# Attention's first chunks in a new order, and state updates issued earlier, in a fused attention and mixture-of-experts kernel

## The chip, the cores and the metric

The kernel runs on one core of a Trainium2 chip, as one program. The metric is the device time of one execution in microseconds (us); a profiled execution gives its own time and, beside it, the span from its first to its last instruction.

## What is computed

Three layers run one after the other. The first is a gated linear attention over 4 batches, 8 heads, 768 steps and heads of 48; its output is 3072 rows of 384. Each row then either skips the second layer or goes to one of 8 experts, and a third layer is applied to all rows.

```python
f = 1.0 / (1.0 + np.exp(-f_logit))
for t in range(S):                                   # attention
    state = f[:, :, t, :, None] * state + k[t] (x) v[t]
    y[:, :, t] = q[:, :, t] . state
out = x                                              # experts, for rows with x @ w_skip > 0
out[i] = x[i] + gate_w[i] * (np.maximum(x[i] @ w1[e], 0) @ w2[e]),   e = argmax(x[i] @ w_gate)
h = x @ w_in; sp = log1p(exp(min(h, 20))) (h where h > 20)           # last layer
return (h * np.tanh(sp)) @ w_out
```

## The kernel before

**Units.** The function `attention` cuts the 24 stretches of 128 steps (6 for each batch) into chunks n = 0 to 23, and each chunk into two halves of two head pairs. A unit d = 2n + h2, 0 to 47, is one such half. All engines get their instructions in the order in which the code stands; each engine works its own queue in order and waits where a tile that it needs is not ready.

**A chunk's preparation**, for all pairs at once: the sigmoid of the gate logits (`sigmoid`, ACT, in place in the tile fb, for three chunks at a time; hh counts these groups of three), then the running product of the gates over the 128 or 384 steps (`scan`, DVE, L303; `chain` joins a chunk of the first group to the one ahead of it and scans its four pairs), then on ACT a logarithm and an exponential (`recip`, L347 and L348: g = 1/e), on DVE three operations (`kg`, two of them, L356 and L357, and `kh`, L364), and on POOL the scaled queries (`qh`, L370). The tile g lies in PSUM and has one buffer. Sigmoid and logarithm are of different tables of ACT, and a change of table (`table`, L656) is an instruction.

**A unit's work.** `stage1(d)` multiplies on PE (tile at, L386) scaled queries and keys and at once turns the keys, copies on ACT and masks either on POOL (`through_act` true: ACT copies all of at into the tile am, L396, and POOL masks it, L399) or on DVE (false: ACT copies the turned keys, L404, and DVE masks the rest, L405). `stage2(d)` makes on PE the outputs (tile ou: L430 from the state tile sbd, L438 from am) and the addition to the state (L450). `evac(d)` copies the outputs on ACT (tile xts, L482). `state(d)` adds on DVE to the state tile (L471, L473 and L475, or L477), and `stage2(d + 2)` needs its result. `finalize(n)` (tile fin, L494) turns a finished chunk and makes its routing numbers.

**Order.** The loop over d issues `state(d - 1)`, the preparation of a chunk that lies ahead, `stage1(d + 2)`, `finalize`, `stage2(d)`, `evac(d)`. Sigmoids and scans of later groups stand at units listed in SIGMOID_AT and SCAN_AT. At units 15, 29, 37, 44 and 46 (the table `group`) `route1` picks experts for a group of chunks with eight small operations on DVE; some units later `rank` counts on PE, `rank_read` takes the counts, `route2_all` makes row numbers, and POOL scatters one chunk's rows per unit (L229). `keep_warm(n)` issues n matmuls of which nothing is used (L664): 25 at the start, 3 after `stage2(0)`, 14 at unit 2. The experts' layers follow the attention, in functions that this change leaves as they are.

```python
SIGMOID_AT = {4: (2, 3), 12: (4, 5), 22: (6, 7)}
SCAN_AT = {4: ((2, 3), (5, 7)), 12: ((3, 5), (7, 9)), 22: ((3, 5), (7, 9))}
group = [(0, 7, 15, 2), (7, 7, 29, 2), (14, 4, 37, 2), (18, 3, 44, 1), (21, 2, 46, 1)]
```

Of the kernel before, what the change touches and what calls it, by code (L numbers as in the profile page):

```python
# [45 lines left out]
WARM = 25  # L46
# [8 lines left out]
LOAD_AT = 24  # L55

# [180 lines left out]
def attention(tc, A, st, weights, open_weights, first_x):  # L237
# [67 lines left out]
    def chain(c):  # L305
        nc.vector.tensor_tensor(d1[0][:, :, c * CH], fb[0][:, :, c * CH], fb[0][:, :, c * CH - 1], ALU.mult)
        for p in range(NP):
            scan(0, p, c, c + 1)
# [34 lines left out]
    def recip(n, parts=1):  # L343
        l = wk.tile([128, NP, CH], F32, name="l", tag="l", bufs=2)[K112]
        g = pr.tile([128, NP, CH], F32, name="g", tag="ut", bufs=1)[K112]
        for ps in pair_parts(parts):
            nc.scalar.activation(out=l[:, ps], in_=e_of(n)[:, ps], func=AF.Ln)  # L347
            nc.scalar.activation(out=g[:, ps], in_=l[:, ps], func=AF.Exp, scale=-1.0)  # L348
        k = wk.tile([128, NP, CH], F32, name="kg", tag="kg", bufs=2)[K112]
        gs[n] = (g, k)  # L350

    def kg(n, ps=slice(0, NP)):
        hh, c3 = divmod(n, 3)
        sl = slice(c3 * CH, (c3 + 1) * CH)
        g, k = gs[n]
        nc.vector.tensor_tensor(k[:, ps], kq[hh % 2][:, 0, ps, sl], g[:, ps], ALU.mult)  # L356
        nc.vector.tensor_tensor(g[:, ps], e_of(n)[:, ps], g[:, ps], ALU.mult)  # L357

    def kh(n, ps=slice(0, NP)):
        g, k = gs[n]  # L360
        if prep[n][1] is None:
            prep[n][1] = wk.tile([128, NP, CH], F32, name="kh", tag="kh", bufs=3)[K112]
        o = prep[n][1]
        nc.vector.scalar_tensor_tensor(o[:, ps], g[:, ps], 2.0, k[:, ps], ALU.subtract, ALU.mult, reverse0=True)  # L364

    def qh(n):
        hh, c3 = divmod(n, 3)
        sl = slice(c3 * CH, (c3 + 1) * CH)
        q = qi[n % 4][K112]
        nc.gpsimd.tensor_tensor(q[:, :, 0:CH], kq[hh % 2][:, 1, :, sl], e_of(n), ALU.mult)  # L370
        prep[n] = [q, None, vb[hh % 3][:, c3, :]]
# [3 lines left out]
    def stage1(d, through_act):  # L375
# [17 lines left out]
        m = part(am, 0, CH)  # L393
        if through_act:
            if keys:
                nc.scalar.copy(am, at)  # L396
            else:
                nc.scalar.copy(m, part(at, 0, CH))
            nc.gpsimd.affine_select(  # L399
                m, m, pattern=[[0, 2], [0, 2], [1, CH]], compare_op=ALU.is_ge, fill=0.0, base=0, channel_multiplier=-1  # L400
            )
        else:
            if keys:
                nc.scalar.copy(part(am, CH, QW), part(at, CH, QW))  # L404
            nc.vector.tensor_tensor(  # L405
                m, part(at, 0, CH), const["mask"].rearrange("p (j a) t -> p j a t", j=2), ALU.mult
            )
        ats[d] = am
# [6 lines left out]
    def stage2(d):  # L415
# [3 lines left out]
        am = ats.pop(d)  # L419
# [26 lines left out]
        if c < NC - 1:  # L446
            for a in range(2):
                for j in range(2):
                    p = 2 * h2 + a
                    nc.tensor.matmul(  # L450
                        ut[64 * j:64 * j + D, a, j * D:(j + 1) * D],
                        lhsT=am[:, j, a * QW + CH:(a + 1) * QW],
                        rhs=vt[:, (2 * p + j) * D:(2 * p + j + 1) * D], start=True, stop=True,
                        skip_group_check=True,
                    )

    def state(d):
        n, h2 = divmod(d, 2)
# [232 lines left out]
    nc.gpsimd.memset(d1[1], E_FLOOR)  # L691
# [27 lines left out]
    for d in range(ND):  # L719
# [5 lines left out]
        fresh = h2 == 0 and 0 < n < NT - 2 and d - 2 not in SIGMOID_AT  # L725
# [3 lines left out]
        if d > 0:  # L729
# [50 lines left out]
        if d == 0:  # L780
            ends(0)
            sigmoid(1, 0, 2)
            sigmoid(1, 2, 4)
            table(LN_EXP)
            starts(1, nc.gpsimd)
            recip(2)
            qh(2)
        if d == 1:
            scan(1, 0)
# [6 lines left out]
            const.update(route_consts(tc, st["cp"], wk))  # L796
        if d % 6 == 1 and d // 6 + 2 < NH:
# [800 lines left out]
```

## Time and profile before

| | us |
|---|---|
| median of 3 runs | 736.2 (733.36 to 737.27) |
| the profiled execution's own time | 732.49 |
| its span | 730.6 |
| PE busy | 692.6 |
| DVE busy | 539.6 |
| ACT busy | 501.2 |
| POOL busy | 170.5 |

The profiled execution was quicker than all three timed runs. The mean granted clock of TensorE over it was 0.972 of full speed. A busy PE says little by itself, since a matmul takes about twice as long at half the clock; the rows below have the granted clock beside the busy time. The attention takes the time up to about 165 us.

### The profile page before, as it was taken

The numbers are of one execution on the slowest core, as the hardware profiler recorded it, in microseconds if no ns is written. First come the engines' busy times: TensorE is split into PE (matmuls) and PEld (weight loads), VectorE is DVE, ScalarE is ACT, GpSimd is POOL, SyncE is SP. The second block draws the span as 40 slices with busy tenths as digits, with TensorE's granted clock in tenths as the row PEclk, the third lists the DMA queues.
The fourth block names the chain that finished last, engine by engine and source line by source line (L and its number), as shares of the span: only waits on it lengthen the run. The fifth ranks groups of instructions, "written<-read, shape, count | busy, mean of one in ns | idle before, by whom it ended". The sixth has DMA issues, their size and how long they took to land.

```text
span 730.6 us, 13087 instructions
## 1 busy us (share of the span) xinstructions
PE 692.6 (95%) x5020; PEld 624.9 (86%) x5021; DVE 539.6 (74%) x1083; ACT 501.2 (69%) x858; POOL 170.5 (23%) x226
## 2 busy tenths in 40 slices
PE   7889798888999999999999999999999999999995
PEld 3678687766999999988899899989989989988994
DVE  7699967985778888969989875666666656666571
ACT  5689675654666663379889867767777676667681
POOL 6644765653011111122223120200020002001002
PEclk8899988899999999999999999999999999999998
DMA  9999844244778974532223022212142224100001
GB/s 210 257 265 273 289 152 130 99 171 147 265 251 272 297 260 149 162 133 72 101 57 118 4 83 87 87 43 87 44 139 79 65 99 141 44 1 23 22 1 47
DMA packets 39286, 95.52 MB, mean 131 GB/s; under 512 B 3540, under 2 KB 28160, under 8 KB 39216
## 3 DMA queue, kind: packets, MB, share of 16 engines
q1 hardware_dynamic: 35120, 82.71, 37.7%
q0 software_dynamic: 4096, 11.90, 4.3%
q8 instruction: 41, 0.67, 0.4%
q14 instruction: 29, 0.24, 0.1%
HBM read 79.53 MB, written 15.84 MB: 131 GB/s over the span
## 4 chain that ended last, share of the span: by engine, by line
PE 81%; DVE 10%; ACT 4%; issue 2%; POOL 1%; DMA 0%; POOLq 0%; ACTq 0%; DVEq 0%
PE y L1130 27%; PE h L1080 27%; PE y L927 9%; PE h L912 8%; DVE fb L303 3%; PE at L386 2%; PE pt L871 2%; PE ou L438 1%; PE h L941 1%; PE fin L494 1%; DVE kh L364 1%; DVE kg L356 1%; DVE g L357 1%; PE ou L430 1%; ACT L656 1%
## 5 line engine op out<-in xcount | busy, mean ns | idle before, releaser
L1094 ACT ACTIVATE sp<-hs 128x512 f32<-128x512 f32 x96 | 59.7, 628 | 72.9 <-DVE hs L1093 72.0
L1080 PE MATMUL h<-wB,wB 128*128 128x512 f32 x432 | 109.1, 397 | 0.0
L1080 PE MATMUL h<-wB,wA 128*128 128x512 f32 x432 | 107.2, 394 | 0.0
L1130 PE MATMUL y<-wD,gh 128*128 128x384 f32 x384 | 98.0, 336 | 0.0
L1130 PE MATMUL y<-wA,gh 128*128 128x384 f32 x384 | 97.7, 335 | 0.0
L1111 DVE TENSOR_TENSOR hs<-hs,sp 128x512 f32<-128x512 f32 x96 | 69.8, 727 | 32.9 <-ACT sp L1105 32.8
L1080 PEld LDWEIGHTS h<-wB,wA 128*128 128x128 f32 x432 | 80.2, 188 | 14.5
L1080 PEld LDWEIGHTS h<-wB,wB 128*128 128x128 f32 x432 | 79.5, 188 | 14.6
L1093 DVE COPY hs<-h 128x512 f32<-128x512 f32 x71 | 48.8, 688 | 40.6 <-PE h L1080 40.4
L1113 DVE TENSOR_TENSOR gl<-hs,gh 128x512 fp32r<-128x512 f32 x96 | 67.3, 701 | 13.1 <-PE y L1130 6.2
L1130 PEld LDWEIGHTS y<-wA,gh 128*128 128x128 f32 x384 | 70.0, 188 | 4.3 <-ACT stage L1149 0.2
L1130 PEld LDWEIGHTS y<-wD,gh 128*128 128x128 f32 x384 | 70.0, 188 | 3.7
L1130 PE MATMUL y<-wD,gl 128*128 128x384 f32 x192 | 64.6, 336 | 0.0
L1130 PE MATMUL y<-wA,gl 128*128 128x384 f32 x192 | 64.5, 336 | 0.0
L1101 ACT ACTIVATE sp<-sp,tiny 128x512 f32<-128x512 f32 x96 | 61.8, 713 | 0.3
L386 PE MATMUL at<-qi,kh 48*128 48x176 f32 (+1 forms) x384 | 44.1, 352 | 10.2 <-DVE lg L502 5.9
L1105 ACT ACTIVATE sp<-sp 128x512 f32<-128x512 f32 x96 | 52.9, 621 | 0.3
L229 POOL DMA_INDIRECT out<-stage,idx x24 | 23.6, 984 | 125.6 <-ACT stage L1149 62.0
L1112 DVE CAST gh<-hs 128x512 fp32r<-128x512 f32 x96 | 48.8, 508 | 3.3
L900 ACT ACTIVATE mhh<-h 128x256 fp32r<-128x256 f32 x64 | 24.6, 384 | 38.4 <-PE h L912 29.7
L386 PEld LDWEIGHTS at<-qi,kh 48*128 48x128 f32 x384 | 31.5, 204 | 15.8 <-POOL am L399 5.4
L229 POOL DMA_INDIRECT tokens<-rows x14 | 15.4, 1098 | 107.1 <-DVE rows L960 104.9
(233 smaller groups left out, 1461.0 us busy)
## 6 DMA issues: line engine op xcount, KB each, us to landing
stage<-in_w SPq DMA_DIRECT2D x64, 768.0 KB
kq<-in_kqT SPq DMA_DIRECT2D x6, 1344.0 KB
rows<-tokens SPq DMA_DIRECT2D x18, 388.0 KB
fb<-in_fT SPq DMA_DIRECT2D x7, 672.0 KB
vb<-in_v SPq DMA_DIRECT2D x7, 576.0 KB
tokens<-zeros SPq DMA_DIRECT2D x4, 776.0 KB
kq<-in_kqT SPq DMA_DIRECT2D x4, 448.0 KB
kq<-in_kqT SPq DMA_DIRECT2D x1, 896.0 KB
```

The lines of the kernel that those rows point to most:

```text
L386: nc.tensor.matmul(at[:, j, a * QW:a * QW + w], lhsT=k[r, p, :], rhs=q[r, p, 0:w], start=True, stop=True)
L912: nc.tensor.matmul(h, lhsT=w[:, o:o + 128], rhs=x[:, k, :], start=(k == 0 and i == 0), stop=(k == KD - 1 and i == 2),)
L927: nc.tensor.matmul(ys[e, a], lhsT=h, rhs=w[:, ws], start=(f == 0 and i == 0), stop=(f == NE - 1 and i == 2),)
L1080: nc.tensor.matmul(h, lhsT=w[:, o:o + 128], rhs=x[:, k, :], start=(k == 0 and i == 0), stop=(k == KD - 1 and i == 2),)
L1093: (nc.scalar.copy if busy(s) else nc.vector.tensor_copy)(hs, h)
L1094: nc.scalar.activation(out=sp, in_=hs, func=AF.Sigmoid, scale=-1.0)
L1101: nc.scalar.activation(out=sp, in_=sp, func=AF.Ln, bias=st["tiny"])
L1105: nc.scalar.activation(out=sp, in_=sp, func=AF.Tanh, scale=-1.0)
L1111: nc.vector.tensor_tensor(hs, hs, sp, ALU.mult)
L1112: nc.vector.tensor_copy(gh, hs)
L1113: nc.vector.tensor_tensor(gl, hs, gh.bitcast(F32), ALU.subtract)
L1130: nc.tensor.matmul(ys[b][a], lhsT=g[:, a * 128:(a + 1) * 128], rhs=w, start=(first and i == 0), stop=(fs[-1] + 1 in ends and i == len(ins) ...
```

## The change

It rearranges the start: chunk 1 is scanned and prepared in two halves of two pairs, the first units' products stand ahead of the second half, the sigmoids of group 1 stand between the copies of unit 2 and unit 0, and chunk 2's scans behind `state(0)`. Units 0 and 2 to 5 (OUT_FIRST) issue `stage2(d)` ahead of `stage1(d + 2)`. The turned keys of units masked on DVE get a tile of their own, kt. The matmuls of `keep_warm` become 18, 4 and 12, and the last stand at unit 3 between `stage2(3)` and `stage1(5)`. At units with scans of later groups `state(d)` is issued between the two scans, and at routing units ahead of `route1`; the call at the next unit then does nothing. The load of the routing weights wg moves ahead of chunk 1's keys on SP's queue, the filling of d1[1] and the building of finw change places on POOL. The line numbers of the changed kernel are 1 to 28 higher.

```diff
@@ constants
-WARM = 25
+WARM = 18
+OUT_FIRST = (0, 2, 3, 4, 5)

-    def chain(c):
-        nc.vector.tensor_tensor(d1[0][:, :, c * CH], fb[0][:, :, c * CH], fb[0][:, :, c * CH - 1], ALU.mult)
-        for p in range(NP):
+    def chain(c, pairs=range(NP)):
+        ps = slice(pairs[0], pairs[-1] + 1)
+        nc.vector.tensor_tensor(d1[0][:, ps, c * CH], fb[0][:, ps, c * CH], fb[0][:, ps, c * CH - 1], ALU.mult)
+        for p in pairs:
             scan(0, p, c, c + 1)
...
-    def recip(n, parts=1):
...
+    def recip(n, which=(slice(0, NP),)):
...
-    def qh(n):
+    def qh(n, ps=slice(0, NP)):
...
         else:
             if keys:
-                nc.scalar.copy(part(am, CH, QW), part(at, CH, QW))
+                kt = wk.tile([128, 2, 2, D], F32, name="kt", tag="kt", bufs=2)
+                nc.scalar.copy(kt, part(at, CH, QW))
...
-                        lhsT=am[:, j, a * QW + CH:(a + 1) * QW],
+                        lhsT=kt[:, j, a, :],
...
     def state(d):
+        if d not in ous:
+            return
...
     def keep_warm(n):
+        wps = pr.tile([128, 512], F32, name="wps", tag="fin", bufs=1)
...
+    wg = load_gate(tc, A["wg9"], wk)
     load_kq(0, 1, 2)
     load_v(0, 1, 2)
-    wg = load_gate(tc, A["wg9"], wk)
...
-    nc.gpsimd.memset(d1[1], E_FLOOR)
+    pairs = pair_parts(2)
...
-    recip(0, 2)
-    chain(1)
+    recip(0, pairs)
+    chain(1, range(0, 2))
     qh(0)
-    for pp in pair_parts(2):
+    const.update(gate_consts(tc, wg, const["ident"], wk))
+    for pp in pairs:
         kg(0, pp)
         kh(0, pp)
-    recip(1)
-    qh(1)
+    recip(1, pairs[0:1])
+    qh(1, pairs[0])
+    stage1(0, False)
+    stage1(1, True)
+    chain(1, range(2, 4))
+    recip(1, pairs[1:2])
+    qh(1, pairs[1])
+    for pp in pairs:
+        kg(1, pp)
+        kh(1, pp)
     table(SIGMOID)
-    stage1(0, False)
     sigmoid(0, 0, NP, 2, 3)
-    kg(1)
-    kh(1)
-    stage1(1, True)
-    const.update(gate_consts(tc, wg, const["ident"], wk))
-    chain(2)
-    for c in (1, 2):
-        nc.gpsimd.memset(d1[0][:, :, c * CH], E_FLOOR)
+    nc.gpsimd.memset(d1[1], E_FLOOR)
...
-        fresh = h2 == 0 and 0 < n < NT - 2 and d - 2 not in SIGMOID_AT
+        fresh = h2 == 0 and 1 < n < NT - 2 and d - 2 not in SIGMOID_AT
...
-        if d > 0:
+        if d > 1:
             state(d - 1)
...
-        if 0 < d and d + 2 < ND:
-            if d == 2:
-                keep_warm(14)
+        ahead = d in OUT_FIRST
+        if d == 1:
+            stage1(3, False)
+        elif not ahead and d + 2 < ND:
             stage1(d + 2, all(d - i not in SIGMOID_AT for i in (1, 2)))
...
         stage2(d)
         if d == 0:
-            keep_warm(3)
-            stage1(2, True)
+            keep_warm(4)
+            stage1(2, False)
+            sigmoid(1, 0, 2)
...
         evac(d)
+        if ahead and d > 0:
+            if d == 3:
+                keep_warm(12)
+            stage1(d + 2, True)
...
                     scan(hh, p)
+                    state(d)
                     scan(hh, p + 1)
...
         if d == 0:
-            ends(0)
-            sigmoid(1, 0, 2)
             sigmoid(1, 2, 4)
             table(LN_EXP)
             starts(1, nc.gpsimd)
+            state(0)
+            chain(2)
+            for c in (1, 2):
+                nc.gpsimd.memset(d1[0][:, :, c * CH], E_FLOOR)
             recip(2)
             qh(2)
+            ends(0)
         if d == 1:
+            state(1)
             scan(1, 0)
...
+        if d == 2:
+            recip(3)
+            qh(3)
+            kg(3)
+            kh(3)
...
             if d == r[2]:
+                state(d)
                 route1(*r[0:2])
```

DVE's queue just behind chunk 0's preparation. Before (d is the scan's second operand, fb the running product, sbd the state):

```order
L405 TENSOR_TENSOR am<-at,mask 128x4x128
L356 TENSOR_TENSOR kg<-kq_100,g 112x512
L357 TENSOR_TENSOR g<-fb_102,g 112x512
L364 SCALAR_TENSOR_TENSOR kh<-g,kg 112x512
L306 TENSOR_TENSOR d_113<-fb_102 112x4
L303 SCALAR_TENSOR_TENSOR fb_102<-fb_102,d_113 112x128 x4
L471 COPY sbd_118<-ou_124 112x4x48
L303 SCALAR_TENSOR_TENSOR fb_103<-fb_103,d_114 112x384 x2
```

and now:

```order
L412 TENSOR_TENSOR am<-at,mask 128x4x128
L308 TENSOR_TENSOR d_113<-fb_102 112x2
L304 SCALAR_TENSOR_TENSOR fb_102<-fb_102,d_113 112x128 x2
L359 TENSOR_TENSOR kg<-kq_100,g 112x256
L360 TENSOR_TENSOR g<-fb_102,g 112x256
L367 SCALAR_TENSOR_TENSOR kh<-g,kg 112x256
L359 TENSOR_TENSOR kg<-kq_100,g 112x256
L360 TENSOR_TENSOR g<-fb_102,g 112x256
L367 SCALAR_TENSOR_TENSOR kh<-g,kg 112x256
L412 TENSOR_TENSOR am<-at,mask 128x4x128
L480 COPY sbd_118<-ou_124 112x4x48
```

Chunk 1's three operations are six of half the size behind the scans of its last two pairs, the mask of unit 2 has come to DVE, and chunk 2's scans stand behind the first state copy.

PE's queue from unit 2 on. Before, behind the 14 unused matmuls (at is `stage1`, fin is `finalize`, ou is `stage2`):

```order
L664 MATMUL wps<-warm 128x512
L386 MATMUL at<-qi_121,kh 128x176 x4
L494 MATMUL fin<-finw,xts_115 64x105 x8
L430 MATMUL ou_124<-qi_120,sbd_118 64x128 x4
L438 MATMUL ou_124<-am,vb_110 48x128 x4
L450 MATMUL ou_124<-vb_110,am 48x48 x4
L386 MATMUL at<-qi_121,kh 128x176 x4
```

and now, behind `stage2(1)`; eleven more pairs of the last kind follow, and then `stage1(5)`:

```order
L457 MATMUL ou_125<-vb_110,am 48x48 x4
L503 MATMUL fin<-finw,xts_115 64x105 x8
L437 MATMUL ou_124<-qi_120,sbd_118 64x128 x4
L445 MATMUL ou_124<-am,vb_110 48x128 x4
L457 MATMUL ou_124<-vb_110,kt 48x48 x4
L391 MATMUL at<-qi_121,kh 128x176 x4
L437 MATMUL ou_125<-qi_120,sbd_118 64x128 x4
L445 MATMUL ou_125<-am,vb_110 48x128 x4
L457 MATMUL ou_125<-vb_110,kt 48x48 x4
L673 LDWEIGHTS warm
L673 MATMUL wps<-warm 128x512
```

Each `stage2` now stands ahead of the `stage1` that it followed, and the unused matmuls stand ahead of `stage1(5)`.

DVE's queue at unit 29, a unit with scans and routing. Before (mx to oh is `route1`):

```order
L303 SCALAR_TENSOR_TENSOR fb_109<-fb_109,d_114 112x384 x2
L540 TENSOR_REDUCE mx<-lg 128x7
L541 TENSOR_SCALAR comp<-lg 128x7
L542 TENSOR_TENSOR rt<-lg,mx 128x56
L543 TENSOR_TENSOR ex<-lg,mx 128x56
L544 SCALAR_TENSOR_TENSOR rt<-rt,iota 128x56
L545 TENSOR_REDUCE mn<-rt 128x7
L546 TENSOR_TENSOR rt<-rt,mn 128x56
L547 TENSOR_TENSOR oh<-rt,comp 128x56
L473 TENSOR_TENSOR ou_125<-ou_125,sbd_117 112x192
L475 TENSOR_TENSOR sbd_118<-ou_125,f_978 112x4x48
L356 TENSOR_TENSOR kg<-kq_101,g 112x512
```

and now:

```order
L304 SCALAR_TENSOR_TENSOR fb_109<-fb_109,d_114 112x384
L482 TENSOR_TENSOR ou_125<-ou_125,sbd_117 112x192
L484 TENSOR_TENSOR sbd_118<-ou_125,f_987 112x4x48
L304 SCALAR_TENSOR_TENSOR fb_109<-fb_109,d_114 112x384
L549 TENSOR_REDUCE mx<-lg 128x7
L550 TENSOR_SCALAR comp<-lg 128x7
L551 TENSOR_TENSOR rt<-lg,mx 128x56
L552 TENSOR_TENSOR ex<-lg,mx 128x56
L553 SCALAR_TENSOR_TENSOR rt<-rt,iota 128x56
L554 TENSOR_REDUCE mn<-rt 128x7
L555 TENSOR_TENSOR rt<-rt,mn 128x56
L556 TENSOR_TENSOR oh<-rt,comp 128x56
```

The two operations of `state(29)` (ou, sbd) have moved up past eight routing operations and the second scan.

## Rows read from the trace of the kernel before

**Rows 1.** Windows: busy us (count) of PE, PEld, DVE, ACT, POOL; granted clock, DMA.
```profile
128.00:146.00 18.00, 15.49 (x221) 13.74 (x217) 16.72 (x46) 12.57 (x26) 11.83 (x14) 0.81 0.28 98
...
250.00:730.60 480.60, 470.90 (x2535) 431.58 (x2533) 340.17 (x604) 332.41 (x527) 59.08 (x65) 0.99 0.26 86
```

**Rows 2.** Windows of PE alone: length, busy us (count), granted clock, DMA share, GB/s.
```profile
14.50:16.30 1.80, 1.43 (x16) 0.50 1.17 239
28.00:30.00 2.00, 2.00 (x25) 0.50 1.09 236
32.00:40.00 8.00, 7.76 (x132) 1.00 1.08 260
114.00:118.00 4.00, 4.00 (x66) 0.50 0.91 235
```

**Rows 3.** DVE in order of time in the opening: start, us, what.
```profile
4.83 1.65 DVE L303 TENSOR_TENSOR_SCAN fb<-fb,d 112x128 f32<-112x128 f32 x4
...
6.78 2.40 DVE L303 TENSOR_TENSOR_SCAN fb<-fb,d 112x128 f32<-112x128 f32 x4
9.10 0.39 DVE L356 TENSOR_TENSOR kg<-kq,g 112x256 f32<-112x256 f32 x1
...
13.84 0.69 DVE L405 TENSOR_TENSOR am<-at,mask 128x512 f32<-128x512 f32 x1 [2.43 <-ACT am L404]
...
24.56 0.66 DVE L356 TENSOR_TENSOR kg<-kq,g 112x512 f32<-112x512 f32 x1
...
26.46 1.79 DVE L303 TENSOR_TENSOR_SCAN fb<-fb,d 112x384 f32<-112x384 f32 x2
...
29.59 0.69 DVE L356 TENSOR_TENSOR kg<-kq,g 112x512 f32<-112x512 f32 x1 [1.08 <-ACT g L348]
...
34.70 0.69 DVE L356 TENSOR_TENSOR kg<-kq,g 112x512 f32<-112x512 f32 x1 [0.81 <-ACT g L348]
```

**Rows 4.** ACT in order of time in the opening.
```profile
11.51 0.60 ACT L348 ACTIVATE g<-l 112x512 f32<-112x512 f32 x1 [1.66 <-DVE kh L364]
...
13.42 0.32 ACT L404 COPY am<-at 128x192 f32<-128x192 f32 x1
...
31.98 0.74 ACT L396 COPY am<-at 128x704 f32<-128x704 f32 x1 [0.62 <-PE at L386]
...
33.40 0.63 ACT L347 ACTIVATE l<-fb 112x512 f32<-112x512 f32 x1
```

**Rows 5.** PE in order of time in the opening.
```profile
16.36 1.06 PE L664 MATMUL wps<-warm 128*128 128x512 bf16 x2 [0.33 <-issue]
...
21.20 3.20 PE L664 MATMUL wps<-warm 128*128 128x512 bf16 x14
26.69 0.87 PE L386 MATMUL at<-qi,kh 48*128 48x176 f32 x8 [2.29 <-DVE kh L364]
```

**Rows 6.** DVE in order of time, from unit 29 to unit 35.
```profile
107.27 2.87 DVE L303 TENSOR_TENSOR_SCAN fb<-fb,d 112x384 f32<-112x384 f32 x2
...
112.02 0.36 DVE L475 TENSOR_TENSOR sbd<-ou,f 112x192 f32<-112x192 f32 x1
...
115.76 0.16 DVE L602 TENSOR_TENSOR pos<-pos,ou 128x7 f32<-128x7 f32 x1 [0.69 <-ACT xts L482]
...
123.15 0.36 DVE L477 TENSOR_TENSOR sbd<-ou,sbd 112x192 f32<-112x192 f32 x1 [1.32 <-ACT xts L482]
124.31 0.69 DVE L356 TENSOR_TENSOR kg<-kq,g 112x512 f32<-112x512 f32 x1 [0.81 <-ACT l L347]
...
128.75 0.69 DVE L356 TENSOR_TENSOR kg<-kq,g 112x512 f32<-112x512 f32 x1 [1.70 <-ACT g L348]
```

**Rows 7.** PE in order of time, behind units 29 and 37.
```profile
112.44 0.66 PE L430 MATMUL ou<-qi,sbd 112*64 112x128 f32 x8 [1.83 <-DVE sbd L475]
...
136.60 0.79 PE L430 MATMUL ou<-qi,sbd 112*64 112x128 f32 x8 [1.99 <-DVE sbd L471]
```

**Rows 8.** POOL in order of time: the first scatter of the second group.
```profile
121.37 1.06 POOL L229 DMA_INDIRECT tokens<-xr,slot  x1 [0.99 <-DVE cs L632]
```

More of the change, by code (lines that the diff above doesn't have):

```diff
@@ L341, in attention @@
     gs = {}
-    def recip(n, parts=1):
-        l = wk.tile([128, NP, CH], F32, name="l", tag="l", bufs=2)[K112]
-        g = pr.tile([128, NP, CH], F32, name="g", tag="ut", bufs=1)[K112]
-        for ps in pair_parts(parts):
+    def recip(n, which=(slice(0, NP),)):
+        if n not in gs:
+            l = wk.tile([128, NP, CH], F32, name="l", tag="l", bufs=2)[K112]
+            g = pr.tile([128, NP, CH], F32, name="g", tag="ut", bufs=1)[K112]
+            gs[n] = (g, wk.tile([128, NP, CH], F32, name="kg", tag="kg", bufs=2)[K112], l)
+        g, _, l = gs[n]
+        for ps in which:
             nc.scalar.activation(out=l[:, ps], in_=e_of(n)[:, ps], func=AF.Ln)
             nc.scalar.activation(out=g[:, ps], in_=l[:, ps], func=AF.Exp, scale=-1.0)
-        k = wk.tile([128, NP, CH], F32, name="kg", tag="kg", bufs=2)[K112]
-        gs[n] = (g, k)
     def kg(n, ps=slice(0, NP)):
@@ L354, in kg @@
         sl = slice(c3 * CH, (c3 + 1) * CH)
-        g, k = gs[n]
+        g, k, _ = gs[n]
         nc.vector.tensor_tensor(k[:, ps], kq[hh % 2][:, 0, ps, sl], g[:, ps], ALU.mult)
@@ L359, in kh @@
     def kh(n, ps=slice(0, NP)):
-        g, k = gs[n]
+        g, k, _ = gs[n]
         if prep[n][1] is None:
@@ L369, in qh @@
         q = qi[n % 4][K112]
-        nc.gpsimd.tensor_tensor(q[:, :, 0:CH], kq[hh % 2][:, 1, :, sl], e_of(n), ALU.mult)
+        nc.gpsimd.tensor_tensor(q[:, ps, 0:CH], kq[hh % 2][:, 1, ps, sl], e_of(n)[:, ps], ALU.mult)
+        if n in prep:
+            return
         prep[n] = [q, None, vb[hh % 3][:, c3, :]]
@@ L393, in stage1 @@
         m = part(am, 0, CH)
+        kt = part(am, CH, QW)
         if through_act:
@@ L407, in stage1 @@
             )
-        ats[d] = am
+        ats[d] = (am, kt)
     ous = {}
@@ L418, in stage2 @@
         q, _, vt = prep[n]
-        am = ats.pop(d)
+        am, kt = ats.pop(d)
         ou = oub[d % 2]
@@ L457, in state @@
     def state(d):
+        if d not in ous:
+            return
         n, h2 = divmod(d, 2)
@@ L659, in attention @@
     nc.vector.memset(warm, 0.0)
-    wps = pr.tile([128, 512], F32, name="wps", tag="fin", bufs=1)
     def keep_warm(n):
+        wps = pr.tile([128, 512], F32, name="wps", tag="fin", bufs=1)
         for i in range(n):
```

## Prediction

> **What bounds the kernel now.** I read the windows over all engines first. From 250 us to the end PE is busy in 470.90 of 480.6 us at a granted clock of 0.99 [rows 1]: the experts' layers are PE at its pace, and this change leaves them alone. Inside the attention it is otherwise. From 128 to 146 us PE is busy for 15.49 of 18 us, but at a clock of 0.81, and DVE for 16.72 [rows 1]. There the end is set by waits that go round PE, ACT and DVE, and by PE's clock. So what the change is worth is what it takes from the attention's length; the rest then starts that much earlier.
>
> Two kinds of places matter. In the opening, chunk 2's `kg` starts at 24.56, chunk 3's at 29.59, chunk 4's at 34.70 [rows 3]. I use these three as posts: from `kg` follow `kh`, `stage1` and all of a unit. Further on, the timeline of PE shows two long idle stretches ended by DVE's state operations: 1.83 us until 112.44 and 1.99 us until 136.60 [rows 7]. The granted clock drops to 0.50 after the first, all through 114 to 118 us [rows 2].
>
> **The opening, part by part.** I work to each post in the new order.
>
> *Chunk 0.* Two of chunk 1's four scans (2.40 us for four) go behind chunk 0's `kg` [rows 3], which can start up to 1.2 us earlier; its six half-size operations last from 9.10 until ACT is released at 11.51, so 2.4 us [rows 3, 4]. I take `kh` done at 10.6 instead of 11.5. The copy that unit 0's mask waits for ran at 13.42, behind an exponential of 0.60 that began at 11.51 and a table change; the mask had waited 2.43 us [rows 3, 4]. The table change now stands behind it, so mask and `stage2(0)` come some 2.3 us earlier. By itself this buys nothing, because `stage1(2)` needs chunk 1's `kh`.
>
> *To chunk 2's `kg`.* DVE's queue from 10.6 holds three masks of 0.69, six short scans of 0.4 to 0.6 (four lasted 1.65, and 2.40 beside POOL), six half operations of 2.4 in all, two state operations of 0.36 and two long scans of 1.79 to 2.87 [rows 3, 6]: 9.4 to 11.7 us. It also waits three times: for the first copy of turned keys (an exponential of 0.60 and a copy of 0.32 less what DVE has in hand, say 0.9); for the second half of chunk 1's logarithm and exponential (half of the size, taken as 0.4 each, and a little to start: 0.9); and, before unit 3's mask, for chunk 2's logarithm, exponential and the copy behind them (0.63 + 0.60 + 0.32 = 1.55) [rows 4]. Sum of waits 3.3, so `kg` at 10.6 + 12.7 to 15.0 = 23.3 to 25.6, before 24.56. I take 24.2, below the middle, since the pair of long scans no longer has chunk 2's `qh` on POOL beside it; that now runs while DVE waits.
>
> *To chunk 3's.* The distance was 29.59 - 24.56 = 5.03. The second state operation no longer stands between (0.36) [rows 3, 6]: 29.59 becomes about 28.9.
>
> *To chunk 4's.* Before, 5.11 us passed between the posts. Its exponential cannot start before chunk 3's `kh`, since g has one PSUM buffer: three operations of 0.69 and one of 0.60 make 2.7, the floor. But ACT's queue has the copy of unit 5 ahead of the logarithm, as before (31.98, which waited for PE, then the logarithm at 33.40 [rows 4]), and unit 5's `stage1` now has the 12 unused matmuls ahead of it. PE: chunk 2's `kh` at 24.2 + 2.0 = 26.2, `stage1(4)` 0.87, `stage2(3)` taken as 0.9 (as `stage1`), the 12 matmuls, `stage1(5)` 0.87. Fourteen such matmuls lasted 3.20, so 12 last 2.74 [rows 5]. `stage1(5)` ends at 31.6; copy 0.74, logarithm 0.63, exponential 0.60 [rows 4] put `kg` at 33.6 to 33.8 instead of 34.70. **Term: -1.0.** Bounds: with the floor alone 28.9 + 2.7 = 31.6, so -3.1. With the 12 at the cost of the pair at 16.36 (0.53 each, at a clock of 0.50 [rows 2, 5]) they last 6.4, so +2.6. I take the 14's price, as these too follow PE work after an idle stretch.
>
> The 7 matmuls fewer at the start cost nothing: PE then waits for chunk 0's `kh`. The routing weights' load ahead of chunk 1's keys delays those by a few small packets, while `kh` of chunk 1 waits for ACT anyway; finw and the filling of d1[1] lie in POOL's idle time, and the fill is ahead of the sigmoids that its reader waits for. Uncovered, a late fill would delay the long scans by its length.
>
> *The separate tile kt* would let DVE mask while ACT copies, if the tile am were all that ties them: the mask had waited 2.43 us for that copy [rows 3]. Both read the same PSUM tile, and in the new program the mask still waits for ACT. [...] Without that tie the first mask could start about 1 us earlier, and `kg` of chunk 2 no more than that. I count 0.
>
> **State ahead of scan and routing.** At unit 29 DVE runs two scans from 107.27 for 2.87 us, eight routing operations, and then the state's two, the second at 112.02 [rows 6]. `stage2(31)` waits for it, 1.83 us, until 112.44 [rows 7]; the first scan ended early in the 2.87 and unit 29's addition was there, so the state could be done by about 109.0. PE then never stops, and need not fall to 0.50. What follows: DVE's read of the counts had waited 0.69, a state operation 1.32, chunk 19's `kg` 0.81 and chunk 20's 1.70, all for ACT behind PE [rows 6]. Those are 4.5 us of DVE idle, and no more than these can go. Against it, `rank` needs the routing's result, which now comes 0.36 + 0.36 later relative to the scans, and the scatters start behind `route2_all`: POOL had waited only 0.99 us for the first, at 121.37 [rows 8]. So bounds -1.0 (POOL sets the pace) to -4.5. I take the DVE waits up to chunk 19's `kg`, 0.69 + 1.32 + 0.81 = 2.8, and 0.3 of chunk 20's: **term -3.1**.
>
> At unit 37 the 1.99 us of PE go too, but DVE is busy for 16.72 of 18 us in 128 to 146 [rows 1] and will not end sooner for that: 0, between -1.5 and 0. Elsewhere a state operation between scans delays the next logarithm by 0.36, three times, and at unit 44 `rank` by as much; a state that is ready earlier gives a like amount back: 0, within 0.7.
>
> **Sum.** 732.49 - 1.0 - 3.1 = 728.4 for the profiled execution. That one was 3.7 us quicker than the median of the runs, 736.2, so a median of **732.1**. I call under 0.5% (3.7 us) no change, about what such runs can tell.
>
> **The rivals.**
> *A, the forecast*, 730.5 to 734: 0.42. Two thirds of it lie beyond 0.5%.
> *B, both terms at their good end and unit 37 too.* PE never drops its clock in either place: -3.1 - 4.5 gives 728.6, with unit 37 727. For it: no row shows a drop where PE had no long idle stretch. Against it: the new opening leaves PE idle while chunk 2's scans run. 0.17, faster.
> *C, given back.* The scatters hold POOL, whose next `qh` and masks stand behind them, so unit 29 gains its 1.0 only, and the opening 0 to 1: 734 to 735.5. For it [rows 8], against it that only the first scatters have no slack. 0.24, no change.
> *D, slower: the unused matmuls at half clock.* Place: PE's queue at unit 3. Between `stage2(1)`, by my working near 18 us, and chunk 2's `kh` at 26 PE has little to do; before, it was idle for 2.29 us ahead of 26.69 and the clock was 0.50 from 28 us on [rows 2, 5]. At 0.53 each the 12 cost 2.6 us more than before's post, and PE is busy for 7.76 of 8 us behind them [rows 2], so half of what follows at half clock is paid as well: over 6 us of it 3 more. 736.2 + 2.6 + 3 - 3.1 = 738.7. It decides if the clock is still 0.50 when the matmuls end. 0.17: two thirds of it slower, the rest within 0.5%. [...]
>
> **Chances.** Faster 0.28 + 0.17 = 0.45; no change 0.14 + 0.24 + 0.06 = 0.44; slower 0.11. Range: from B's 727 to D's lower half, 738.
>
> **What would show it.** Right: PE without idle time at units 30 and 31 and a clock of 1.00 there; chunk 4's `kg` near 33.7; chunk 19's near 120.5. Wrong: the 12 matmuls longer than 4 us; the posts up to chunk 4 later than before; a new wait of PE for POOL's `qh` or masks around chunk 20; the second scan of a split pair slower than before for POOL beside it.

## The result and the profile after

The changed kernel is slower: median 736.74 us (734.18 to 741.47, 20 runs) beside 733.37 us (728.65 to 737.27, 20 runs) for the kernel before, ratio 1.0052 [1.0034, 1.0069]. That is 3.4 us more; the forecast was 4.1 us less (732.1 from 736.2, the median of three runs). The profiled execution took 736.31 us with a span of 734.4 us, 3.8 more than the span of before.

The windows over all engines, with the columns of [rows 1], show that the experts are where they were: PE busy in 474.69 of 484.4 us at 0.99. In PE's timeline the first matmul on the weights wC starts at 193.98 instead of 190.34, and the span ends 3.8 us later: the loss lies ahead of that.

```profile
128.00:146.00 18.00, 15.28 (x213) 13.29 (x210) 14.22 (x34) 12.35 (x25) 15.74 (x17) 0.81 0.33 112
250.00:734.40 484.40, 474.69 (x2562) 435.31 (x2560) 343.19 (x610) 334.79 (x532) 62.08 (x67) 0.99 0.26 88
```

DVE's timeline of the changed kernel shows the posts: chunk 2's `kg` where it was forecast (24.2), chunk 3's 1.1 us late, chunk 4's 3.2 us late and 2.2 behind before [rows 3], after a wait of 4.40 us for ACT.

```profile
24.25 0.66 DVE L359 TENSOR_TENSOR kg<-kq,g 112x512 f32<-112x512 f32 x1
...
29.96 0.69 DVE L359 TENSOR_TENSOR kg<-kq,g 112x512 f32<-112x512 f32 x1 [1.92 <-ACT g L353]
...
36.91 0.69 DVE L359 TENSOR_TENSOR kg<-kq,g 112x512 f32<-112x512 f32 x1 [4.40 <-ACT g L353]
```

ACT's timeline shows what the logarithm and the exponential of these two posts stood behind: both times a copy of turned keys that waited for PE.

```profile
28.02 0.75 ACT L402 COPY am<-at 128x704 f32<-128x704 f32 x1 [3.10 <-PE at L391]
...
34.97 0.75 ACT L402 COPY am<-at 128x704 f32<-128x704 f32 x1 [4.39 <-PE at L391]
35.61 0.63 ACT L352 ACTIVATE l<-fb 112x512 f32<-112x512 f32 x1
36.28 0.60 ACT L353 ACTIVATE g<-l 112x512 f32<-112x512 f32 x1
```

And PE's timeline shows what the second copy waited for. From 30.09 to 34.05 PE runs unused matmuls, 3.96 us (eleven of the 12 are in the trace), while `stage1(5)` stands behind them.

```profile
26.39 1.54 PE L391 MATMUL at<-qi,kh 48*128 48x176 f32 x8 [1.88 <-DVE kh L367]
27.86 1.12 PE L437 MATMUL ou<-qi,sbd 112*64 112x128 f32 x8
...
29.62 0.53 PE L457 MATMUL ou<-vb,kt 128*48 128x48 f32 x8
30.09 0.61 PE L673 MATMUL wps<-warm 128*128 128x512 bf16 x1
30.91 3.21 PE L673 MATMUL wps<-warm 128*128 128x512 bf16 x10 [0.22 <-issue]
34.05 0.87 PE L391 MATMUL at<-qi,kh 48*128 48x176 f32 x8
```

The windows of PE (columns of [rows 2]) give the granted clock there, and at units 29 to 40: 0.50 from 24 to 32 us, where `stage1(4)` took 1.54 us, and 1.00 from 34 on, where `stage1(5)` took 0.87; 1.00 from 112 to 124, where before had 0.50 from 114 to 118 [rows 2], but 0.60 just ahead of that, from 108 to 112; and a dip to 0.57 from 134 to 142, which is not new: before has 0.50 from 138 to 142.

```profile
24.00:32.00 8.00, 5.90 (x46) 0.50 1.09 235
32.00:34.00 2.00, 2.00 (x8) 0.82 1.08 220
34.00:40.00 6.00, 6.00 (x97) 1.00 1.09 215
108.00:112.00 4.00, 4.00 (x44) 0.60 0.00 0
112.00:124.00 12.00, 10.89 (x212) 1.00 0.48 122
134.00:142.00 8.00, 6.56 (x56) 0.57 0.52 173
```

At unit 31 PE no longer waits for the state, as forecast (before: 1.83 us, [rows 7]). But PE's timeline has two new waits further on, ahead of the key products of chunks 19 and 20, and POOL's timeline names what is late: `qh`, queued behind the scatters.

```profile
129.61 0.87 PE L391 MATMUL at<-qi,kh 48*128 48x176 f32 x8 [0.81 <-POOL qi L373]
...
135.44 1.55 PE L391 MATMUL at<-qi,kh 48*128 48x176 f32 x8 [1.91 <-POOL qi L373]
```

```profile
130.77 1.01 POOL L230 DMA_INDIRECT tokens<-xr,slot  x1 [0.17 <-issue]
131.81 0.65 POOL L405 TENSOR_SCALAR_AFFINE_SELECT am<-am 128x512 f32<-128x512 f32 x1
132.62 0.99 POOL L230 DMA_INDIRECT tokens<-xr,slot  x1 [0.17 <-issue]
133.63 1.76 POOL L373 TENSOR_TENSOR qi<-kq,fb 112x512 f32<-112x512 f32 x1
```

### The profile page after: what moved, and what is told of

It reads as the page before. It is cut to its first block, busy times and chain, and to the rows that moved or that the text cites. A ratio compares the mean times of both kernels' runs of the same rounds, so it can differ in the third digit from the quotient of the medians.

```text
span 734.4 us, 13070 instructions
## 1 busy us (share of the span) xinstructions
PE 692.2 (94%) x5011; PEld 623.7 (85%) x5013; DVE 541.0 (74%) x1088; ACT 502.0 (68%) x860; POOL 171.7 (23%) x226
## 4 chain that ended last, share of the span: by engine, by line
PE 80%; DVE 8%; ACT 3%; POOL 3%; issue 2%; DMA 2%; POOLq 0%; SPq 0%; DVEq 0%; ACTq 0%
PE y L1158 27%; PE h L1108 27%; PE y L955 9%; PE h L940 8%; DVE fb L304 2%; PE at L391 2%; PE pt L899 2%; PE fin L503 1%; POOL tokens L230 1%; PE ou L445 1%; PE ou L437 1%; POOL am L405 1%; PE h L969 1%; DVE kh L367 1%; DVE g L360 1%
## 5 line engine op out<-in xcount | busy, mean ns | idle before, releaser
L230 POOL DMA_INDIRECT out<-stage,idx x24 | 23.8, 991 | 124.1 <-ACT stage L1177 61.1
L928 ACT ACTIVATE mhh<-h 128x256 fp32r<-128x256 f32 x64 | 24.7, 385 | 38.1 <-PE h L940 30.1
```

## The experiments

Each time is compared with that of the kernel before on the same chip. The table has, beside the ratio, distances in us between the starts of `kg` of two chunks, each the difference of two rows of DVE's timeline: they show a stretch by itself, whatever went before. Each comes from one profiled execution, and executions differ: before, e7, e10 and e11 run the same instructions up to unit 29, and their 3 to 4 are 5.11, 6.60, 6.47 and 3.52. "Old" and "new" are the openings, "12" the unused matmuls at unit 3, "all" and "29" where the state stands between scans (everywhere, with routing; or at unit 29 alone), "DVE" that `qh` of chunks 19 and 20 runs there.

| kernel | what it is | ratio, 95% interval | 3 to 4 | 5 to 6 | 12 to 13 | 16 to 19 | 19 to 23 |
|---|---|---|---|---|---|---|---|
| before | old | 1 | 5.11 | 9.58 | 4.37 | 19.72 | 23.95 |
| changed | new, 12, all | 1.0052 [1.0034, 1.0069] | 6.95 | 10.57 | 5.13 | 17.51 | 25.36 |
| e1 | new, all | 1.0009 [0.9987, 1.0032] | 3.18 | 10.59 | 5.11 | 17.51 | 25.51 |
| e2 | new, 16 elsewhere, all | 1.0064 [1.0041, 1.0087] | 2.75 | 10.59 | 5.12 | 17.53 | 26.46 |
| e3 | old, all | 1.0013 [0.9990, 1.0035] | 3.52 | 10.10 | 5.12 | 17.54 | 26.62 |
| e4 | new, 12 | 1.0039 [1.0013, 1.0065] | 6.30 | 10.04 | 4.37 | 19.92 | 24.53 |
| e5 | new, 8 elsewhere, all | 1.0014 [0.9991, 1.0037] | 3.23 | 10.60 | 5.12 | 17.53 | 26.61 |
| e6 | old, all, DVE | 0.9993 [0.9968, 1.0018] | 3.52 | 10.11 | 5.13 | 18.15 | 23.21 |
| e7 | old, DVE | 0.9987 [0.9959, 1.0014] | 6.60 | 9.58 | 4.37 | 18.00 | 23.52 |
| e8 | old, all, scatters later | 1.0069 [1.0035, 1.0102] | 3.52 | 10.10 | 4.68 | 19.03 | 25.91 |
| e9 | old, 12 | 1.0017 [1.0001, 1.0033] | 8.54 | 9.57 | 4.37 | 17.19 | 25.43 |
| e10 | old, 29 | 0.9999 [0.9980, 1.0017] | 6.47 | 9.59 | 4.38 | 16.90 | 26.49 |
| e11 | old, 29, DVE | 0.9969 [0.9947, 0.9991] | 3.52 | 9.58 | 4.38 | 17.26 | 23.69 |
| e12 | new, 29, DVE | 0.9967 [0.9944, 0.9989] | 3.66 | 10.07 | 4.37 | 17.90 | 23.49 |

**e1, without the 12.**

```diff
-            if d == 3:
-                keep_warm(12)
             stage1(d + 2, True)
```

> The changed kernel without the 12 unused matmuls ahead of unit 5's stage1. Theory H (the opening loses because PE runs at half clock ahead of unit 5, and the 12 unused matmuls stand on the path there for 4.0 us): unit 5's stage1 starts near 30 instead of 34.05 and lasts about 1.5 at half clock, chunk 4's kg comes near 33.5 instead of 36.91, the clock is full some us later than without the cut, and the time is 733 to 735. Rival N (the 12 are what brings the clock back, so taking them out only moves the loss): chunk 4's kg near 33.5 too, but the granted clock stays near 0.50 until 38 us or later, chunk 6's kg stays near 50, and the time is 736 to 738.

Measured 733.97 us, 1.0009 against 1.0052 with the 12: as theory H has it, they cost 0.43% or 3.1 us (both intervals together leave some 2 us either way). Its timeline of DVE has chunk 4's `kg` 3.68 us sooner, and its windows of PE show the clock back without them. Over all runs the mean granted clock is alike, 0.971 in the changed kernel's 20 and 0.972 in e1's 12, so over a whole run little of the 3.1 us can be the clock's.

```profile
30.05 0.69 DVE L359 TENSOR_TENSOR kg<-kq,g 112x512 f32<-112x512 f32 x1 [1.93 <-ACT g L353]
...
33.23 0.69 DVE L359 TENSOR_TENSOR kg<-kq,g 112x512 f32<-112x512 f32 x1 [0.63 <-ACT g L353]
```

```profile
20.00:30.00 10.00, 7.20 (x72) 0.50 1.11 246
30.00:32.00 2.00, 2.00 (x30) 0.85 1.10 245
32.00:34.00 2.00, 1.72 (x33) 1.00 1.08 228
```

By the time rival N falls. In this profile one thing that both expected falls too: the clock is full earlier than with the 12, not later, behind the real work of units 4 and 5. But that is one execution, the quickest of the 12. e12 further down has the same opening without the 12, and there the clock was 0.50 until 36 us, as N has it, with chunk 4's `kg` at 34.63 and chunk 6's at 49.56. So what the 12 do to the clock is not shown; what they cost in time is. The windows of PE of e12:

```profile
18.00:30.00 12.00, 8.74 (x84) 0.50 1.13 225
30.00:36.00 6.00, 6.00 (x64) 0.50 1.10 229
36.00:38.00 2.00, 2.00 (x26) 0.72 1.09 233
```

**e2 and e5, the unused matmuls where PE is idle.** e2 has 10 ahead of unit 2's output and 6 ahead of `stage1(4)`; e5 has 8 at the first place alone. The diff is that of e2; e5 has keep_warm(8) in the first piece and no keep_warm in the second.

```diff
+        if d == 2:
+            keep_warm(10)
         if h2 == 0 and 1 <= n < NT - 2:
             finalize(n - 1)
...
-            if d == 3:
-                keep_warm(12)
+            if d == 2:
+                keep_warm(6)
             stage1(d + 2, True)
```

> The changed kernel with the 12 unused matmuls taken from ahead of unit 5's stage1, and 10 put ahead of the output of chunk 0 in unit 2 and 6 ahead of unit 4's stage1, where PE was idle for 2.99 and 1.88 us. Theory H: PE has no idle stretch over 1 us from 16 to 30 us, the granted clock is 1.00 from 22 to 34, unit 4's stage1 lasts 0.87 instead of 1.54, chunk 4's kg comes at 32 to 33.5, chunk 6's at 46 to 47.5, and the time is 732 to 734. Rival O (the new order itself is longer, whatever the clock: chunk 4's kg waits for ACT and the one buffer of g): chunk 4's kg at 35 or later at a clock of 1.00, time 736 to 737.

> The changed kernel without the 12 unused matmuls ahead of unit 5's stage1, and with 8 of them ahead of the output of chunk 0 in unit 2, where PE was idle for 2.99 us. Theory H (what the new opening lacks is PE's clock): the granted clock is 1.00 from 24 us on, unit 4's stage1 starts near 26.4 and lasts 0.87 instead of 1.54, chunk 3's kg comes near 29.2, chunk 4's at 31.8 to 32.5 (33.23 without any of the 12), chunk 6's at 45.5 to 46.5, and the time is 731 to 733.5. Rival W (unused matmuls do not pay at any place, the opening is bound by ACT and DVE): chunk 4's kg at 33 or later although the clock is 1.00, time 733 to 735.

e2: 738.04 us, a miss for both. The second block writes the PSUM buffer of the logits (`fin`), so it waited 1.94 us for DVE to read them, behind two scans, and `stage1(4)` behind it came at 29.23 instead of 26.39. My edit made the new delay. The clock was 1.00 from 24 to 50 us, as H asks, and chunk 3 to 4 took 2.75, the shortest of all; chunk 3's `kg` came only at 32.14, so e2 does not tell what the clock alone is worth. PE's timeline of e2:

```profile
27.85 1.46 PE L673 MATMUL wps<-warm 128*128 128x512 bf16 x6 [1.94 <-DVE lg L511]
29.23 0.87 PE L391 MATMUL at<-qi,kh 48*128 48x176 f32 x8
```

e5 put the posts where H wanted them (29.03, 32.26, chunk 6's at 46.03), though the clock was 1.00 only to about 27 us. But its 731.79 us, which as a number lie in H's range, stand against 731.55 for before on this chip, where the chip of e1 to e4 had given 733.79. By the ratio e5 is no better than e1: the time is rival W's, though not W's posts. What was won until chunk 7 (`kg` at 51.08) was gone at chunk 8 (58.04, a distance of 6.96 against 4.15 in the changed kernel), since the clock fell behind another idle stretch, ahead of unit 10's product. A row of PE's timeline, and its window:

```profile
48.19 1.55 PE L391 MATMUL at<-qi,kh 48*128 48x176 f32 x8 [2.94 <-DVE lg L511]
```

```profile
48.00:60.00 12.00, 11.81 (x96) 0.50 1.07 297
```

**e3 and e4, the two parts of the change by themselves.** e3 adds to the kernel before these lines (and the early return of `state`); e4 takes them out of the changed kernel:

```diff
                     scan(hh, p)
+                    state(d)
                     scan(hh, p + 1)
...
             if d == r[2]:
+                state(d)
                 route1(*r[0:2])
```

> The kernel before with only the state operations moved: between the two scans of a pair and ahead of the routing. Theory P (the state moves take PE's wait at unit 31 away, but POOL's scatters start no earlier and give it back): chunk 6's kg within 0.6 of 47.02, no wait of PE over 0.5 us before unit 31's stage2, chunk 19's kg at 121.5 to 123, then a wait of PE for POOL's qh of 1 to 2 us before chunk 22's key product and half clock behind it, chunk 23's kg within 1 of 148.26, and the time within 1.5 us of before. Rival S (the state operations between scans are what makes the changed kernel slower): time 2 to 4 us above before, with chunk 6's kg 0.5 to 1 later and more of it added at each group of scans. By the prediction's own term it would be 3.1 us below before.

> The changed kernel with the state operations back at their old places in the scans and the routing (behind both scans, behind route1), so that it has the new opening alone. Theory H: chunk 4's kg near 36.9 and chunk 6's near 49.7, as far behind the kernel before as in the changed kernel, PE's idle stretch of about 2 us before unit 31's stage2 is back, and the time is 735 to 738. Rival S: chunk 4's kg as in the changed kernel but the end within 1 us of before.

e4 with 1.0039 and e3 with 1.0013 add up to the whole, each with some 0.25% either way. The opening makes most of the loss; the states give nothing (-0.7 to +2.6 us by e3's interval), where the prediction had -3.1 us. e4 is as theory H has it: chunk 4's `kg` at 36.05, chunk 6's at 48.86, and PE's wait ahead of unit 31's output back at 2.47 us. In e3 the way to chunk 19 is 2.2 us shorter and that from 19 to 23 2.7 longer, with PE's waits for POOL of 0.39 and 1.45 us (ahead of chunks 19 and 20, not 22 as expected); chunk 6's `kg` came at 45.72, 1.3 earlier than expected, since this execution had the clock at 1.00 from 24 to 48. Rival S is right in part: all kernels with "all" need 10.10 or 10.11 us instead of 9.57 to 9.59 from chunk 5 to 6 in the old opening (10.57 to 10.60 instead of 10.04 to 10.07 in the new) and 5.11 to 5.13 instead of 4.37 from 12 to 13 (e8, where the scatters move, apart). DVE's timeline of the changed kernel shows why: the second pair's last scan stands behind two states; ACT's logarithm (48.96) waits 0.97 us for it, and `kg` for ACT.

```profile
45.56 2.19 DVE L304 TENSOR_TENSOR_SCAN fb<-fb,d 112x384 f32<-112x384 f32 x2
47.67 0.32 DVE L486 TENSOR_TENSOR sbd<-ou,sbd 112x192 f32<-112x192 f32 x1
47.92 0.94 DVE L304 TENSOR_TENSOR_SCAN fb<-fb,d 112x384 f32<-112x384 f32 x1
50.25 0.69 DVE L359 TENSOR_TENSOR kg<-kq,g 112x512 f32<-112x512 f32 x1 [1.39 <-ACT g L353]
```

**e6, e7 and e8, POOL relieved.** e6 (on e3) and e7 (on before):

```diff
-        nc.gpsimd.tensor_tensor(q[:, :, 0:CH], ...)
+        eng = nc.vector if n in (19, 20) else nc.gpsimd
+        eng.tensor_tensor(q[:, :, 0:CH], ...)
```

e8 (on e3) issues each scatter behind the next unit's `qh`:

```diff
-                    scatter(r[0] + i)
+                    held.append(r[0] + i)
...
             qh(n + 2)
+        while held:
+            scatter(held.pop(0))
```

> The kernel before with the state operations moved, and the qh of chunks 19 and 20 on DVE instead of POOL (0.7 us each there instead of 1.3 to 1.8). Theory P (POOL's scatters, with qh queued behind them, take back what the state moves give): PE's waits for POOL's qh ahead of the key products of chunks 19 and 20 (0.39 and 1.45 with the moves alone) go, chunk 21's and 22's kg come 1 to 2.5 us earlier against chunk 18's than with the moves alone, and the time is 1 to 2.5 us below the kernel with the moves alone. Rival C (something else, DVE or the clock, sets the pace there): the distance from chunk 18's kg to chunk 22's stays within 0.7 of 26.2, no change of time.

> The kernel before with the qh of chunks 19 and 20 on DVE instead of POOL and nothing else. Theory P: there PE waits for DVE's states and not for POOL, so that 1.4 us more on DVE help nothing: the distance from chunk 18's kg to chunk 22's is 24.7 as before or up to 1.4 longer, the time the same or up to 1.5 us above before. Rival C: as much gain here as in the kernel that has the states moved too.

> The kernel before with the state operations moved, and each scatter issued one unit later, behind that unit's qh on POOL, so that qh of chunks 19 and 20 has one scatter less ahead of it. Theory P: qh of chunks 19 and 20 end about 1 us earlier, PE's two waits shrink from 0.39 and 1.45 to 0 and 0.5, chunk 22's kg comes about 1 us earlier against chunk 18's than with the moves alone (26.2), and the time is 0.5 to 1.5 us below it. Rival C: no change from it.

In e6 the waits for POOL's `qh` at chunks 19 and 20 are gone and chunk 18 to 22 takes 23.37 us instead of 26.17: theory P's mechanism. Its time, 1.5 us better than e3 by the ratios, is not told apart from it. In e8 that distance is 25.00, 1.2 less, as P says, but the time is 0.69% above before: the edit holds back the last scatters too, and from chunk 23's `kg` to the first transposes of gathered rows it takes 12.58 us instead of e3's 11.12. From chunk 11 to 12 it takes 7.73 instead of 6.49, with PE waiting 2.72 us for DVE ahead of a product; what made that stretch long stays open. e7 was to be no shorter than before; it was 1.5 us shorter from 18 to 22, and by their times e6 and e7 are alike, as rival C has it. It also holds the row that tells most about unit 29, first PE's timeline, then the window:

```profile
112.44 0.66 PE L431 MATMUL ou<-qi,sbd 112*64 112x128 f32 x8 [1.83 <-DVE sbd L476]
```

```profile
112.00:124.00 12.00, 11.02 (x202) 1.00 0.67 182
```

The wait for the state is the one of [rows 7], to the hundredth. In before the clock was 0.50 behind it, here it stays 1.00, and chunk 16 to 19 takes 18.00 us instead of 19.72, with `qh` added on DVE and the states at their old places.

**e9, the 12 added to before**, with the PSUM tile allocated in each call as in the changed kernel:

```diff
             if d == 2:
                 keep_warm(14)
+            if d == 3:
+                keep_warm(12)
```

> The kernel before with 12 more unused matmuls ahead of unit 5's stage1 and nothing else. Theory T (unused matmuls at that place stand on the path to chunk 4's kg, whatever the order around them): chunk 4's kg comes 2 to 4 us later against chunk 3's than the 5.1 of before, and the time is 2 to 4 us above before, as much as taking them out of the changed kernel gave. Rival N (they matter only in the new order, or give back through the clock what they take): within 1 us of before.

734.50 against 733.52 us, by the ratio slower by 1.2 us (0.1 to 2.4): T's direction, with less than its 2 to 4. In PE's timeline they last 2.75 us, at a clock of 1.00 from 24 to 40: the forecast's price within 0.01. They also waited 2.27 us for the logits' read, and chunk 3 to 4 took 8.54 us, which is 2.75 + 2.27 + the 3.52 of this stretch at full clock without them. So on the path they cost time at full clock as well. Where the rest came back I could not tell apart from the clock's dips further on.

```profile
30.76 2.75 PE L664 MATMUL wps<-warm 128*128 128x512 bf16 x12 [2.27 <-DVE lg L502]
33.44 0.87 PE L386 MATMUL at<-qi,kh 48*128 48x176 f32 x8
```

e9 also tells something of unit 29. Its states and its `qh` are where before has them, yet it reaches chunk 19 in 17.19 us, with 0.48 us of waiting for the state ahead of unit 31's output, and then it has the changed kernel's waits for POOL (0.81 and 1.91 us there) and a 19 to 23 as long as there (25.43). PE's timeline of e9, ahead of the key products of chunks 19 and 20:

```profile
126.08 0.87 PE L386 MATMUL at<-qi,kh 48*128 48x176 f32 x8 [0.81 <-POOL qi L370]
131.91 1.55 PE L386 MATMUL at<-qi,kh 48*128 48x176 f32 x8 [1.92 <-POOL qi L370]
```

So the wait for POOL does not come from the state moves: it also meets a chunk 19 that came early without them.

**e10, e11 and e12, the states at unit 29 alone**; e11 adds the edit of e6, and e12 is the changed kernel with all that (no 12, states at 29, `qh` on DVE).

```diff
                     scan(hh, p)
+                    if d == 29:
+                        state(d)
                     scan(hh, p + 1)
```

> The kernel before with the state operation between the two scans at unit 29 only, and every other state where it was. Theory Q (the early splits cost: the second scan ends later and PE's idle stretch before unit 10's key product grows from 1.75 to 2.3 to 2.9 us; unit 29's own gain is given back behind POOL): that stretch is 1.75 again, the distance from chunk 16's kg to chunk 19's is 17.5 to 18 (19.72 before), that from chunk 19's to chunk 23's 25 to 26.6 (23.95 before), and the time is 0.5 to 1.5 us below the kernel with all state moves, that is within 1.5 of before. Rival G (nothing gives unit 29's gain back but the early splits): 2 to 3 us below before.

> The kernel before with the state operation between the scans at unit 29 only and the qh of chunks 19 and 20 on DVE. Theory P (POOL gives unit 29's gain back): the distance from chunk 16's kg to chunk 19's is 17.5 to 18.2 and from chunk 19's to chunk 23's 23 to 24, together 41 to 42 instead of 43.67, and the time is 1.5 to 3 us below before. Rival C (with qh on DVE the order of the states no longer matters): 41.5 as in the kernel with qh on DVE alone, time within 1 us of before.

> The changed kernel without the 12 unused matmuls, with the state operation between the scans at unit 29 only and not ahead of the routing, and the qh of chunks 19 and 20 on DVE: the changed kernel without what each theory holds against it. Theory H with P: chunk 4's kg near 33.2, chunk 6's at 46 to 47, chunk 19's to chunk 23's 23 to 24, and the time is 1.5 to 4 us below before. Rival W (the new opening without the 12 is worth nothing, and with qh on DVE the states are not either): within 1 us of before.

e10 is as fast as before (0.9999), with the shortest way to chunk 19 (16.90, below Q's 17.5 to 18) and one of the longest from there to 23 (26.49): rival G falls, Q stands. With `qh` on DVE (e11) the second distance is 23.69 and the kernel 0.31% faster than before. PE's timelines of e10 and of e11 show the wait for POOL ahead of chunk 20's key product (1.45 us), the 0.45 us for DVE that e11 has in its place, and a wait for DVE's state that e11 has further on, ahead of an output:

```profile
128.62 0.87 PE L386 MATMUL at<-qi,kh 48*128 48x176 f32 x8 [1.45 <-POOL qi L370]
```

```profile
125.03 0.87 PE L387 MATMUL at<-qi,kh 48*128 48x176 f32 x8 [0.45 <-DVE lg L505]
...
130.10 0.66 PE L431 MATMUL ou<-qi,sbd 112*64 112x128 f32 x8 [1.48 <-DVE sbd L474]
```

The time is P's, but e7's interval overlaps e11's: how much of it is the state and how much `qh` the times do not settle. The distances speak for `qh`. The last two columns add up to 42.6 to 44.9 in the ten kernels with `qh` on POOL, whatever their states, and to 41.0 to 41.5 in the four with it on DVE, e7 with its states at the old places (41.52) among them; so the state move adds no more than some 0.6 to it in these profiles, which is rival C's reading. e12 missed theory H's posts (chunk 4's `kg` at 34.63, chunk 6's at 49.56) and equals e11, so the new opening without its 12 is worth nothing measurable (-0.02%, with some 0.3% either way). Both beat both kernels, by 0.3% and 0.8%.

## Why the prediction was wrong

**Opening, term -1.0: the step that failed.** "Fourteen such matmuls lasted 3.20, so 12 last 2.74" priced work that stands ahead of `stage1(5)` by a row at full clock; they took 3.96, at 0.50 up to 32 us and 0.82 up to 34. And the forecast's `stage1(4)` and `stage2(3)`, to be done at 28.0, ended at 30.1 at half clock; some 0.3 of that the clock did not make, since the text took `stage2` for 0.9 and it lasts 1.2 at full clock too (27.27 to 28.49 in e9). Together 3.3 us, which is chunk 4's 36.91 instead of 33.6; chunk 3's `kg` came 1.1 late the same way, behind a copy that waited for `stage1(4)`. The bound for exactly this (+2.6) was in the text, as was rival D; I chose the other end "as these too follow PE work after an idle stretch", while the rows that D named, 2.29 us of idle PE and 0.50 from 28 us on [rows 2, 5], spoke for D.

D foresaw the place and the low clock there, but it needed a clock of 0.50 still when the matmuls end, and that was 1.00 from 34 us on, so the 3 us that it counted behind them did not come. Its 738.7 is near by luck: it had +5.6 for the opening and -3.1 for the states where 3.1 and 0.9 were measured, and a base of 736.2 where 20 runs of before gave 733.37. By that base too the 736.74 fell within the range of 727 to 738. Nor is the clock the whole cause: e9 loses with them at 1.00, and e5 with none there and better posts gains nothing. What is shown is that the 12 on that path cost 3.1 us in the new order, with some 2 us either way.

**The post they were credited against.** The -1.0 was measured from 34.70, chunk 4's `kg` of one execution in which PE ran at 0.50 from 28 to 30 us [rows 2]. Seven profiles of the old opening without the 12 stand between 31.58 and 36.21: four at 31.6 to 32.3, with chunk 3 to 4 in 3.52, three at 34.7 or more with the clock down near 30 (0.50 from 28 to 30 in before and in e10). So the 3.1 us by which the forecast's floor (31.6, without the 12) beat that post are what a full clock gives the old order too; e12 against e11 shows that nothing was left. Chunk 2's `kg`, forecast at 24.2 from 24.56, is of the same kind: it starts at 23.0 to 23.8 in six of the eight profiles of the old opening, and at 24.0 to 25.3 in all six of the new one, so the new order is no earlier there. The two late ones, before and e7, are the ones in which POOL's first `qh` ran beside chunk 1's four scans, which then took the 2.40 us of [rows 3]; in the other six POOL started it behind them, and they took 1.37. So one of the prices that the opening was worked out from holds in two executions of eight. POOL's timeline of before, then DVE's and POOL's of e10, which has the same instructions there:

```profile
7.55 1.35 POOL L370 TENSOR_TENSOR qi<-kq,fb 112x512 f32<-112x512 f32 x1
```

```profile
6.80 1.37 DVE L303 TENSOR_TENSOR_SCAN fb<-fb,d 112x128 f32<-112x128 f32 x4
8.49 1.29 POOL L370 TENSOR_TENSOR qi<-kq,fb 112x512 f32<-112x512 f32 x1 [1.00 <-ACT g L348]
```

**Unit 29, term -3.1.** PE's wait for the state went, and chunk 19's `kg` came 2.2 us earlier against chunk 16's. That the clock then stays up did not follow: it was 1.00 from 112 to 124, but 0.60 from 108 to 112, and with the same move 0.57 from 114 to 118 in e3. The size was wrong twice. The waits added up (0.69 + 1.32 + 0.81) were mostly the clock's work in one execution: e7 with the same 1.83 us wait and e9 with the old order reach chunk 19 in 18.00 and 17.19. And with the states moved and `qh` on POOL, chunk 19 to 23 takes 1.4 to 2.7 us more, as PE waits there for POOL's `qh` behind the scatters: rival C's place, and the wait the text named. e9, which has the old order, loses 1.5 there in the same way. C's price was wrong, since it had the gain stop at 1.0 rather than be won and then lost.

**"Elsewhere 0, within 0.7."** Mis-sized: the early states cost 0.52 from chunk 5 to 6 and 0.75 from 12 to 13. With e3's other fixed differences to before (6 to 7: 5.65 for 5.89; 9 to 10: 9.61 for 9.33; 11 to 12: 6.49 for 6.40) that makes 1.4 us, with the 0.24 that came back from 6 to 7 taken off.

**Right:** chunk 2's `kg` as a number; unit 37 at 0 (its 1.99 us of waiting for DVE are gone, and 1.91 for POOL stand ahead of chunk 20's key product); the experts left alone. No run shows the 0 for kt by itself, since none has the new order without kt; what DVE's timeline of the changed kernel shows is that the first mask still waits 0.83 us for ACT's copy into kt. The sum of what was measured, 3.1 for the 12, 0.9 for the states (e3) and 0 for the rest, is 4.0, against 3.8 in the spans and 3.4 in the medians; each of these terms has some 2 us either way, so the close sum is partly luck.

## What to carry to other kernels

A matmul that computes nothing is work like any other: the 12 took 2.75 us in e9 at a clock of 1.00, and 3.96 in the changed kernel at 0.50 and then 0.82. Look at what stands behind it on PE and who waits for that, and price it at the clock that the rows ahead of it show. A wait that sits beside a clock dip in one profile is not worth the dip (with the same 1.83 us of waiting chunk 16 to 19 took 19.72 us in before and 18.00 in e7); look at the same stretch in a second profile before its length becomes a term. When a wait is taken from one engine, follow the next queue: here POOL's scatters with `qh` behind them were the next bound, for the old order as well, and only the kernels that moved `qh` off POOL passed chunks 16 to 23 in less than 42 us.

## What the runs showed of the hardware

The same instructions with the same idle time are not always followed by the same clock. Behind 1.83 us of idle PE ahead of unit 31's output the granted clock fell to 0.50 in before and stayed 1.00 in e7; behind 2.94 us ahead of unit 10's product it fell in e5 (0.50 from 48 to 60) and not in e1, where that product starts at 49.21 and lasts 0.87 (the two differ by 8 unused matmuls near 20 us). e3 and e6 have the same instructions up to chunk 19, and behind 2.28 us ahead of that product it fell in e3 (0.50 from 50 to 52) and stayed 1.00 in e6. The same holds from run to run: over the 35 runs of before beside e1 to e4 the mean granted clock goes from 0.966 to 0.987, and the slower runs have the lower clock (correlation -0.81). By these rows one profile cannot price a dip. In the old opening, chunk 3 to 4 took 3.52 us in e11, with the clock at 1.00 from 24 to 40 us, and 6.47 in e10, with 0.50 from 26 to 30 and 0.55 from 30 to 32: 3.0 us, nearly the whole loss of 3.4.
